# Splitting the last output stores of an attention and gated-MLP kernel

## The chip, the cores and the metric

The kernel runs on one core of a Trainium2 chip. The metric is the device time of one execution in microseconds. Three runs of the kernel before gave 410.19, 409.29 and 409.55 us, median 409.55.

## What is computed

For four sequences of 768 tokens, eight heads of width 64: softmax attention, in which a token sees 8 global positions and the 96 before it, with a bias that grows with distance. Its output x (512 wide) goes through a gated MLP, and x is added to the result:

```
h = gelu(x @ w_in)                       # 512 -> 1024, tanh form
u, v = h[..., :512], h[..., 512:]
v_n = (v - mean) / sqrt(var + 1e-6) * g_ln
v_s = w_sg @ v_n + b_sg                  # mixes the 768 tokens
out = x + (u * v_s) @ w_out              # float32
```

## The kernel before

The output is kept transposed: 512 rows (features) by 768 columns (tokens) for each sequence. `out_tile` makes one tile of it, 128 rows (feature block `m`, 0 to 3) by 384 columns (token chunk `c`, 0 or 1): 32 tiles in all. Matmuls work on float32 values split into a high and a low part, three for each of the four steps of the contraction (lines 547 to 549), and add up in a PSUM tile `mm_ps`. When the last step is done, VectorE adds x and writes the tile `o` in SBUF (line 670), and SyncE stores `o` with one DMA (line 676): 128 rows of 1,536 bytes. All stores and loads are issued by SyncE.

Each step is an `Op` of a plan. `Plan.order` simulates the engines with fixed costs (for a store: SP, 0.38 us) and a table of shifts, and writes the instructions of each engine down in that order, so an operation's callback may issue several instructions, but the plan counts only the costs that stand beside it.

The end of the kernel is the last sequence's second chunk, which is marked `last`. There x's two parts are added into `o` ahead (line 662), so that after the matmuls one add is left. Line 1326 sets the order: the steps of tiles `m` = 0, 1, 2 are interleaved, so that these three end one shortly after the other, and tile `m` = 3 follows on its own:

```
phase([], [t[k] for k in range(KD) for t in o[1][:3]] + o[1][3])
```

Behind the plan, line 1335 loads a flag on each engine and line 1336 branches over a general path that these inputs don't need. At that point SyncE waits for eight DMA counters, one wait each; the closing of the program (shown as line 1481) waits for eight again, and then all engines meet in a barrier.

Of the kernel before, what the change touches and what calls it, by code (L numbers as in the profile page):

```python
# [15 lines left out]
ALU = mybir.AluOpType  # L16
PSUM = bass.MemoryType.PSUM

P = 128
# [5 lines left out]
KD = DM // P  # L25
CH = 384
# [20 lines left out]

PATIENCE = 2.0

HINTED = ("DVE", 40, mybir.EngineType.DVE), ("PE", 30, mybir.EngineType.PE)  # L50

IDLE, ON_UNTIL = 0.3, 75.0
# [99 lines left out]
def on_dve(n, more=0.0):  # L152
    return "DVE", 0.065 + n / 960 + more, 0.155 + n / 960 + more


def on_dve_sb(n, more=0.0):

    return "DVE_SB", 0.065 + n / 960 + more, 0.155 + n / 960 + more
# [7 lines left out]
def on_pool(n, more=0.0):  # L166
    return "POOL", 0.05 + n / 390 + more, 0.08 + n / 390 + more
# [41 lines left out]
def parts(used):  # L209

    return [(b.buf, b.part) if isinstance(b, View) else b if isinstance(b, tuple) else (b, None)
            for b in used]
# [18 lines left out]
class Now:  # L231
# [5 lines left out]
    def op(self, ways, reads=(), writes=()):  # L237
        for b, _ in parts(writes):
            if b.kind and b.tile is None:
                n = self.next[b.kind] = self.next.get(b.kind, -1) + 1  # L240
                b.slot = n % self.places[b.kind]
        ways[0][-1]()


class Plan:
# [247 lines left out]
    def emit(self, start):  # L493
# [5 lines left out]
        todo = self.search(start)  # L499
        hinted = {[o for o in todo if o.way[0] == e][-n]: t for e, n, t in HINTED}  # L500
        for o in todo:
# [22 lines left out]
class Moe:  # L524
# [128 lines left out]
    def out_tile(self, x, c, m, dst, last=False):  # L653
        nc, w, op, gt = self.nc, self.w, self.plan.op, self.gt
        cs = slice(c * CH, (c + 1) * CH)
        ms = slice(m * P, (m + 1) * P)

        whole = self.temp("o", CH) if last else None

        def ahead(first):  # L660
            xm = x[m][c]
            both = lambda eng: eng.tensor_tensor(whole.ap, xm[:, 0, :].bitcast(F32),
                                                 xm[:, 1, :].bitcast(F32), ALU.add)
            op([on_dve_sb(CH) + (lambda: both(nc.vector),),
                on_pool(CH) + (lambda: both(nc.gpsimd),)], [xm], [whole], [first])

        def after(ps):
            o, xm = whole or self.temp("o", CH), x[m][c]
            with_x = lambda: o.ap if last else xm[:, 0, :].bitcast(F32)
            op([on_dve(CH) + (lambda: nc.vector.tensor_tensor(  # L670
                o.ap, ps.ap, with_x(), ALU.add),)], [ps, xm], [o])
            if not last:
                lo = lambda eng: eng.tensor_tensor(o.ap, o.ap, xm[:, 1, :].bitcast(F32), ALU.add)  # L673
                op([on_dve_sb(CH) + (lambda: lo(nc.vector),),
                    on_pool(CH) + (lambda: lo(nc.gpsimd),)], [xm], [o])
            op([("SP", 0.38, 0.7, lambda: nc.sync.dma_start(dst[ms, cs], o.ap))], [o], [])

        return self.terms(
            KD, CH, lambda k: ((w.wout[:, 0, k, ms], w.wout[:, 1, k, ms]),
                               (gt[c, k][:, 0, :], gt[c, k][:, 1, :])),  # L680
            lambda k: [gt[c, k], (w.wout, (k, m // 2))], 1, after, ahead if last else None)
# [803 lines left out]
```

## Time and profile before

| | |
|---|---|
| median of three runs | 409.55 us |
| the profiled execution | 409.76 us |
| its span, first to last instruction | 407.9 us |
| PE busy | 396.8 us (97%) |
| VectorE busy | 321.8 us (79%) |
| ScalarE busy | 216.8 us (53%) |
| output stores | 32, of 192 KB each |

Times inside the profile count from the start of the span. The rows come from one profiled execution. "SPq" is SyncE's queue of DMA issues and waits, which count as no busy time. A DMA's landing is the time from its issue until its counter says that all of it has arrived.

### The profile page before, as it was taken

The page shows a single profiled execution, that of the slowest core. Times are in us where ns is not written, and L with a number is a line of the kernel's source. Part 1 is how long each engine was busy: PE and PEld are TensorE (multiplying, and loading weights), DVE is VectorE, ACT ScalarE, POOL GpSimd, SP SyncE. Part 2 cuts the span into 40 slices and gives each one's busy share as a digit, 9 for nine tenths or more (in the row PEclk, how much of TensorE's full clock was granted, in tenths as well). Part 3 has the DMA queues.
Part 4 walks back from the last instruction along what each step waited for, and adds up shares of the span by engine and source line. Part 5 has one row for each costly group of instructions (what it writes and reads, how often), then busy time and mean ns, then how long its engine had stood idle before and what let it go on. Part 6 is the DMA issues. An engine that isn't in the chain of part 4 may idle for free.

```text
span 407.9 us, 12436 instructions
## 1 busy us (share of the span) xinstructions
PE 396.8 (97%) x4593; PEld 360.9 (88%) x4593; DVE 321.8 (79%) x1088; ACT 216.8 (53%) x726; POOL 184.0 (45%) x332
## 2 busy tenths in 40 slices
PE   7889999999999999999999999999999999999995
PEld 4667778899998989899999888999999888999995
DVE  7998999999978999877667899866667668764372
ACT  5999999875646855545333565642333234400110
POOL 3324553373557676666456445553456142403200
PEclk9999999999999999999999999999999999999998
DMA  7874765236777886655887872753676501001002
GB/s 232 282 221 129 216 209 147 95 106 209 244 240 224 256 271 203 183 165 168 252 241 237 249 233 82 202 147 129 190 240 189 168 19 40 0 2 57 23 0 82
DMA packets 50033, 67.12 MB, mean 165 GB/s; under 512 B 5808, under 2 KB 33968, under 8 KB 49968
## 3 DMA queue, kind: packets, MB, share of 16 engines
q1 hardware_dynamic: 49968, 66.28, 52.9%
q8 instruction: 37, 0.61, 0.6%
q14 instruction: 28, 0.23, 0.2%
HBM read 47.91 MB, written 18.35 MB: 162 GB/s over the span
## 4 chain that ended last, share of the span: by engine, by line
PE 85%; DVE 10%; issue 1%; DMA 1%; ACT 1%; POOL 0%; POOLq 0%
PE mm_ps L547 24%; PE mm_ps L549 23%; PE mm_ps L548 23%; PE av L1043 7%; PE s_ps L894 6%; PE tps L1015 2%; DVE p L926 1%; DVE stage L719 1%; DVE stage L717 1%; DMA stage<-in_w_in_dram 1%; DVE p L956 1%; DVE st L605 1%; DVE vg L571 1%; DVE win L724 1%; DVE stage L715 1%
## 5 line engine op out<-in xcount | busy, mean ns | idle before, releaser
L931 ACT ACTIVATE p<-p,pst 128x168 f32<-128x168 f32 (+1 forms) x192 | 80.9, 425 | 28.8 <-DVE pst L926 23.7
L953 POOL TENSOR_SCALAR p<-p,pst 128x168 f32<-128x168 f32 (+1 forms) x137 | 57.2, 434 | 27.8 <-DVE pst L944 27.4
L547 PE MATMUL mm_ps<-wsg,z 128*128 128x384 f32 x192 | 65.0, 339 | 0.0
L549 PE MATMUL mm_ps<-wsg,z 128*128 128x384 f32 x192 | 64.3, 335 | 0.1
L548 PE MATMUL mm_ps<-wsg,z 128*128 128x384 f32 x192 | 64.2, 334 | 0.0
L926 DVE CUSTOM_DVE_ANT_0 p<-s_ps,bias 128x168 f32<-128x168 f32 (+1 forms) x192 | 53.5, 318 | 6.7 <-PE s_ps L894 5.2
L673 POOL TENSOR_TENSOR o<-o,x 128x384 f32<-128x384 f32 x28 | 28.7, 1023 | 52.5 <-DVE o L670 39.0
L1043 PE MATMUL av<-pt,v 64*64 64x128 f32 (+1 forms) x1408 | 47.9, 251 | 1.4 <-DVE pt L1021 1.1
L1043 PEld LDWEIGHTS av<-pt,v 64*64 64x64 f32 x1408 | 36.8, 134 | 10.2 <-issue 5.3
L547 PE MATMUL mm_ps<-x,win 128*128 128x384 f32 x128 | 43.9, 343 | 0.0
L547 PE MATMUL mm_ps<-gt,wout 128*128 128x384 f32 x128 | 43.0, 336 | 0.0
L548 PE MATMUL mm_ps<-gt,wout 128*128 128x384 f32 x128 | 43.0, 336 | 0.0
L549 PE MATMUL mm_ps<-gt,wout 128*128 128x384 f32 x128 | 42.9, 335 | 0.0
L549 PE MATMUL mm_ps<-x,win 128*128 128x384 f32 x128 | 42.8, 335 | 0.0
L548 PE MATMUL mm_ps<-x,win 128*128 128x384 f32 x128 | 42.8, 334 | 0.0
L566 ACT ACTIVATE u<-mm_ps 128x384 f32<-128x384 f32 x32 | 15.6, 488 | 45.7 <-PE mm_ps L549 45.2
L547 PE MATMUL mm_ps<-win,x 128*128 128x512 f32 x96 | 39.5, 411 | 0.0
L894 PE MATMUL s_ps<-qk 64*64 64x64 f32 (+2 forms) x1408 | 39.0, 242 | 0.1
L549 PE MATMUL mm_ps<-win,x 128*128 128x512 f32 x96 | 37.7, 393 | 0.0
L548 PE MATMUL mm_ps<-win,x 128*128 128x512 f32 x96 | 37.7, 392 | 0.0
L894 PEld LDWEIGHTS s_ps<-qk 64*64 64x64 f32 x1408 | 34.0, 135 | 3.9 <-issue 2.7
L547 PEld LDWEIGHTS mm_ps<-wsg,z 128*128 128x128 f32 x192 | 36.0, 188 | 1.4 <-issue 0.9
(112 smaller groups left out, 900.7 us busy)
## 6 DMA issues: line engine op xcount, KB each, us to landing
qk<-in_qk_in_dram SPq DMA_DIRECT2D x32, 328.0 KB, 4.1
pt<-far SPq DMA_DIRECT2D x24, 384.0 KB, 4.8
v<-in_v_in_dram SPq DMA_DIRECT2D x32, 256.0 KB, 4.1
out_dram<-o SPq DMA_DIRECT2D x32, 192.0 KB, 2.2
far<-tt SPq DMA_DIRECT2D x48, 96.0 KB, 1.9
far<-stage SPq DMA_DIRECT2D x48, 96.0 KB, 2.3
qk<-in_qk_in_dram SPq DMA_DIRECT2D x16, 276.0 KB, 3.7
v<-in_v_in_dram SPq DMA_DIRECT2D x16, 192.0 KB, 4.1
```

What stands on the lines that cost most here:

```text
L547: mm(ps.ap, ah, bh, start=(i == 0), stop=False)
L548: mm(ps.ap, ah, bl, start=False, stop=False)
L549: mm(ps.ap, al, bh, start=False, stop=(i == n - 1))
L566: op([on_act(n) + (lambda: nc.scalar.activation(out.ap, h.ap, AF.Square, scale=math.sqrt(GELU_C * GELU_A)),)], [h], [out])
L571: op([on_dve(n) + (lambda: nc.vector.scalar_tensor_tensor(out.ap, out.ap, 1.0, h.ap, ALU.add, ALU.mult),)], [h], [out])
L673: lo = lambda eng: eng.tensor_tensor(o.ap, o.ap, xm[:, 1, :].bitcast(F32), ALU.add)
L894: nc.tensor.matmul(s_ps[h][e * HQ:(e + 1) * HQ, i * W + c0:i * W + c0 + n], qk[rows, qc:qc + HQ], qk[rows, QW + k0:QW + k0 + n], start=Tru ...
L926: nc.vector.tensor_tensor_reduce(out=p[:, g, cols], in0=s_ps[h][:, i * W:i * W + nk], in1=bias[:, 2 * j + h, w0:w0 + nk], op0=ALU.add, op1 ...
L931: op([on_act(nk, 0.225) + (lambda p=p, g=g, cols=cols, i=i: nc.scalar.activation(p[:, g, cols], p[:, g, cols], AF.Exp, bias=st[:, 0, i, g: ...
L953: op([on_pool_ts(nk, -0.10) + (partial(scaled, lambda o, a, c: nc.gpsimd.tensor_scalar(o, a, c, 1.0, ALU.mult, ALU.mult)),), on_act(nk, 0. ...
L1015: nc.tensor.transpose(tps[:, a * P:(a + 1) * P], pc[:, c:c + P], ident)
L1043: nc.tensor.matmul(to, v[rows, vc:vc + D], of, stop=True, skip_group_check=True, **kw)
```

## The change

The last tile (`m` = 3 of the last chunk of the last sequence, `ending`) is added in two instructions of 192 columns and stored in two DMAs of 192 columns, 128 rows of 768 bytes each. The stores of the other three tiles of that chunk are issued in parts by rows: tile 0 in three (rows 0 to 41, 42 to 84, 85 to 127), tiles 1 and 2 in two (64 rows each). All other tiles are added and stored as before. The costs that the planner sees are unchanged.

```diff
+STORED_IN = {0: 3, 1: 2, 2: 2}
...
             o, xm = whole or self.temp("o", CH), x[m][c]
             with_x = lambda: o.ap if last else xm[:, 0, :].bitcast(F32)
-            op([on_dve(CH) + (lambda: nc.vector.tensor_tensor(
-                o.ap, ps.ap, with_x(), ALU.add),)], [ps, xm], [o])
+            ending = last and m == KD - 1
+            some = [slice(0, CH // 2), slice(CH // 2, CH)] if ending else [slice(0, CH)]
+
+            def add():
+                for s in some:
+                    nc.vector.tensor_tensor(o.ap[:, s], ps.ap[:, s], with_x()[:, s], ALU.add)
+
+            def store():
+                for s in some:
+                    nc.sync.dma_start(dst[ms, c * CH + s.start:c * CH + s.stop], o.ap[:, s])
+
+            def in_parts(n):
+                for h in range(n):
+                    rows = slice(h * P // n, (h + 1) * P // n)
+                    nc.sync.dma_start(dst[m * P + rows.start:m * P + rows.stop, cs], o.ap[rows])
+
+            op([on_dve(CH) + (add,)], [ps, xm], [o])
...
-            op([("SP", 0.38, 0.7, lambda: nc.sync.dma_start(dst[ms, cs], o.ap))], [o], [])
+            op([("SP", 0.38, 0.7, partial(in_parts, STORED_IN[m]) if last and m in STORED_IN else store)], [o], [])
```

## Rows read from the trace of the kernel before

**Rows 1.** The page: span, busy time of the engines, chain by engine.

```profile
span 407.9 us, 12436 instructions
...
PE 396.8 (97%) x4593; PEld 360.9 (88%) x4593; DVE 321.8 (79%) x1088; ACT 216.8 (53%) x726; POOL 184.0 (45%) x332
...
PE 85%; DVE 10%; issue 1%; DMA 1%; ACT 1%; POOL 0%; POOLq 0%
```

**Rows 2.** Timeline of the last adds: start, duration (us), instruction, [idle before].

```profile
400.33 1.60 DVE L670 TENSOR_TENSOR o<-mm_ps,o 128x384 f32<-128x384 f32 x3 [2.24 <-PE mm_ps L549]
...
403.08 0.34 PE L549 MATMUL mm_ps<-gt,wout 128*128 128x384 f32 x1
403.45 0.56 DVE L670 TENSOR_TENSOR o<-mm_ps,o 128x384 f32<-128x384 f32 x1 [1.06 <-PE mm_ps L549]
```

**Rows 3.** Timeline of SyncE: the four stores of the last chunk.

```profile
400.92 0.33 SPq L676 DMA_DIRECT2D out_dram<-o  x1
...
401.44 0.33 SPq L676 DMA_DIRECT2D out_dram<-o  x1
...
401.96 0.33 SPq L676 DMA_DIRECT2D out_dram<-o  x1
...
404.04 0.33 SPq L676 DMA_DIRECT2D out_dram<-o  x1
```

**Rows 4.** DMA view of 404.5 to 406: 40 slices (busy tenths, GB/s), packets by queue.

```profile
DMA  0000000000786979969799764105700000000000
GB/s 0 0 0 0 0 0 0 0 0 0 287 328 246 573 287 410 451 246 614 287 369 492 287 206 123 41 0 219 218 0 0 0 0 0 0 0 0 0 0 0
DMA packets 146, 0.21 MB, mean 142 GB/s; under 512 B 16, under 2 KB 144, under 8 KB 144
...
q1 hardware_dynamic: 144, 0.20, 35.4%
q14 instruction: 2, 0.02, 3.3%
```

**Rows 5.** Line 676: issues (ns min/median/max) of all stores, then of the last chunk.

```profile
L676 SPq DMA_DIRECT2D out_dram<-o x32: 332/344/1202, 107.6 to 404.0; - x32
...
L676 SPq DMA_DIRECT2D out_dram<-o x4: 332/332/333, 400.9 to 404.0; - x4
...
DMA to landing us min/median/max: 1.9/1.9/2.1
```

**Rows 6.** Lines 1336 and 1481: SyncE's waits at the end, first and last start.

```profile
L1336 SPq EVENT_SEMAPHORE  x2: 17/17/17, 404.9 to 405.0; - x2
...
L1336 SPq EVENT_SEMAPHORE  x6: 17/17/17, 406.2 to 406.5; - x6
...
L1481 SPq EVENT_SEMAPHORE  x8: 28/28/28, 406.6 to 407.0; - x8
...
L1481 SPq EVENT_SEMAPHORE  x10: 17/28/28, 406.6 to 407.8; - x10
```

**Rows 7.** Timeline of SyncE near 314: four issues in a row, and the first.

```profile
314.32 1.75 SPq L990 DMA_DIRECT2D far<-tt  x4
...
314.32 0.30 SPq L990 DMA_DIRECT2D far<-tt  x1
```

**Rows 8.** Groups by form, VectorE: adds of two widths; busy us, mean ns.

```profile
L1119 DVE TENSOR_TENSOR x<-av,x 128x128 fp32r<-128x128 f32 x56 | 12.7, 282 | 0.1
...
L670 DVE TENSOR_TENSOR o<-mm_ps,o 128x384 f32<-128x384 f32 x4 | 2.2, 558 | 3.3 <-PE mm_ps L549 3.3
```

**Rows 9.** Stretches while the last four stores transfer; the last columns are DMA share, GB/s.

```profile
core 0: us, PE busy (x) PEld busy (x) DVE busy (x) ACT busy (x) POOL busy (x), PEclk, DMA share, GB/s
...
402.50:403.00 0.50, 0.50 (x5) 0.50 (x4) 0.00 (x0) 0.00 (x0) 0.00 (x0) 1.00 1.02 372
...
405.00:405.30 0.30, 0.00 (x0) 0.00 (x0) 0.00 (x0) 0.00 (x0) 0.00 (x0) 1.00 1.03 389
```

**Rows 10.** A stretch in which only rows of 768 bytes are transferred (as before).

```profile
315.50:316.00 0.50, 0.50 (x8) 0.25 (x6) 0.39 (x1) 0.00 (x0) 0.00 (x0) 1.00 0.83 206
```

## The prediction

> **What bounds the kernel now.** I read the page's engine totals first: PE is busy for 396.8 us of a 407.9 us span, and PE lines make up 85% of the chain of waits [rows 1]. Then the end of that chain, since the change touches nothing before it: the last matmuls and one VectorE add, which ends at 403.45 + 0.56 = 404.01 [rows 2]. There the chain as listed stops, but the span goes on for 3.9 us. The other views say what fills it. SyncE issues the last store at 404.04 [rows 3]. Its packets start about 0.83 us later: in the DMA slices of 404.5 to 406 (each 0.0375 us wide) the first busy one begins at 404.87, and the store's packets end about 405.5 [rows 4]. The slowest of the four stores takes 2.1 us from issue to landing, so it has landed at about 404.04 + 2.1 = 406.14 [rows 5]. SyncE waits at the kernel's end for eight counters, one after another: two of these waits are over by 405.0, six run off only from 406.2 to 406.5; then eight more and the closing barrier go to 407.9 [rows 6]. So the last 4 us are add, issue, transfer, landing, waits, barrier, each on the path. No matmul is left to hide anything, and whatever store lands last sets the time.
>
> The span stands in an execution of 409.76 us; the median of the runs shown is 409.55. I sum against the profiled one and take off the 0.21 at the end.
>
> **The change, part by part.**
>
> *More issues on SyncE.* Four stores become nine. A store issued after a wait takes 0.33 us [rows 3]; issues that follow one another at once are slower: four in a row take 1.75 us, the first 0.30, so (1.75 - 0.30)/3 = 0.48 a step [rows 7]. I take 0.38 for the first step (0.33 and a gap of 0.05) and 0.48 for the rest; 0.38 for all is the other end. The parts of tile 0 are issued at 400.92, 401.30 and 401.78, those of tiles 1 and 2 from 402.26 to 403.70, and SyncE is free at 404.18 instead of waiting for the last add. The add itself: a 128x384 add takes 558 ns and a 128x128 one of the same operation 282 ns [rows 8], so 1.08 ns a column and 351 ns for 192 columns. Adds back to back step by (1.60 - 0.56)/2 = 0.52 us [rows 2], so by 0.52 - 0.21 = 0.31 at half width. The second half ends 0.31 + 0.35 = 0.66 us after the start, 0.10 later than now, the first half 0.21 earlier. Behind these adds VectorE has only its share of the ending. The halves of tile 3 go out at 404.18 and 404.66, so the last issue is 0.62 later than 404.04. With 0.38 a step SyncE is free in time and the last issue is at about 404.22, 0.18 later.
>
> *Transfers.* Between 405.0 and 405.3 the 16 engines carry 389 GB/s with nothing idle, 24.3 GB/s each, so a row of 1,536 bytes takes 63 ns (66 by the 372 GB/s of 402.5 to 403.0) [rows 9]. Rows of 768 bytes, in the stage of the small transfers, run at 206 GB/s with a share of 0.83: 206/0.83/16 = 15.5 GB/s, 50 ns a row [rows 10]. Half the columns is not half the time: 8 half-rows take 0.40 us against 0.50 for 8 whole ones.
>
> *How the rows are shared out.* This decides. The last store shows 144 packets, of which 16 are under 512 bytes: 128 rows and one closing packet for each of 16 engines, and with all 16 busy to the end these are equal shares of 8 rows [rows 4, 9]. Tile 0 is now cut at rows 42 and 85, into 42, 43 and 43 rows. No transfer of the trace has such a count, so I bound it. Spread over 16 engines as now, 43 rows are at most 3 rows an engine, 0.19 us. On one engine they are 43 x 63 ns = 2.7 us, twice. Which row is nearer? What the rows show is equal shares, and 43 is prime: it has no equal share below 43 engines except all on one. I take the upper end, and keep the lower for the range.
>
> By the row alone, read as "always 16 engines", the sum would be about +0.1 us. The Trainium skill ("DMA: Bandwidth & Descriptors", section "Why a DMA increments its semaphore by 16 and not by 1") speaks against this change: a store from SyncE runs on the largest number of engines, up to 16, that divides the count of the slowest dimension on both sides, and 127 partitions go to one engine. By it 42 rows go to 14 engines and 43 to one, which gives the sum below; no run here shows it, since every count in the trace divides by 16.
>
> *The sum with one engine for each 43-row part.* I assume that both parts go to the same engine, and that this one also has its share of every later store, in order of issue. It starts at 401.30 + 0.83 = 402.13 (its share of the 42 rows is done by then). It carries 86 rows (5.42 us), 4 of 64 rows from each of four parts of tiles 1 and 2 (16 x 63 ns = 1.01) and 8 half-rows from each half of tile 3 (16 x 50 ns = 0.80): 7.23 us, so it is done at 409.36. The late issues above are covered by this queue, and so is the slower add. From the last packet to the landing I take 0.44: a landing of 1.9 us, the median of the four [rows 5], would have come at 405.94, after packets that end about 405.5. Landing at 409.80 against 406.14: +3.66.
>
> *The waits at the end.* The counters are taken in turn, and the wait on the last store is now third of eight; five more stores would make it the eighth. The five waits behind it, of (406.5 - 406.2)/5 = 0.06 us each or a little more by the rounded row [rows 6], are then over before the landing; I take 0.33. That stores take the counters in the order of the waits is inferred; otherwise this is 0.
>
> Sum: +3.66 - 0.33 = +3.33. 409.76 + 3.33 - 0.21 = 412.88; the 63 ns may hold moments in which an engine had not started, so I round down to 412.8. Its own range: 60 ns a row (-0.3), if the 63 hold such starts, gives 412.5; 66 ns a row (+0.3) and a landing of 0.77 after the last packet, as the store of 2.1 us would have it (+0.33), give 413.5.
>
> **Rivals.**
>
> *All 16 engines share any count* (not slower). Then 42 or 43 rows cost what they cost now, the first store's data leave a little earlier to no use, and the end is set by SyncE: last issue 0.62 later, its rows 0.10 shorter, five waits fewer (0.33): +0.19; with 0.38 a step (0.18 in place of 0.62) it is -0.25. Between them 409.3 to 409.75, about 409.5: no change. Instruction fetches run beside the last store (two packets of another queue, [rows 4]), and the landing of 2.1 against 1.9 may be theirs; free of them it is 0.2 less, 409.1. For it: 389 GB/s shows that the sharing works well. Against it: nothing shows unequal shares. It decides at about 31 rows: an engine with fewer of tile 0's last two parts than that (31 x 63 ns + the 1.81 of the later stores = 3.76 us from 402.13) is done by 405.89, when the last half-rows would be anyway (404.66 + 0.83 + 0.40).
>
> *The pile-up also blocks the issue.* One store of this line took 1.20 us to issue against a median of 0.34 [rows 5], so SyncE can be held up. If it is held until the full engine has drained, the last halves start a first-packet delay later: 0.83 more, 413.6. For it: 86 rows are far more than any engine has queued in the ending now. Against it: an engine that always has work loses nothing by a late issue, and SyncE needs to be ahead by one part only.
>
> *The halves don't work as halves.* If the first half's store waited for both adds, it would be issued at 403.45 + 0.66 + 0.03 = 404.14, when SyncE is not yet free. Worth nothing in either case.
>
> **How the numbers follow.** One engine for 43 rows 0.64 (412.8), the same with blocked issue 0.08 (413.6), shared by 16 0.22 (409.5), something that the rows don't show 0.06. A measurement of this kernel can tell about 0.2%, 0.82 us, from no change. The first two are slower; the third stays within 0.82 us on both sides, even with the 0.2 of the fetches; a gain of 0.82 us is in no sum, 0.05 of the rest. The range runs from the rival's 409.1 to 413.6.
>
> **What the profile after would show.** Right: DMA share near one sixteenth, some 24 GB/s, for several us after 403; a landing of over 5 us for stores of line 676's successor; SyncE's last wait at about 409.8 and none after it before the final eight; VectorE done at about 404.1 and PE unchanged. Wrong: the DMA share falls to zero by 406, all landings near 2 us; then the shares are not equal ones. If the last wait is still followed by five of 0.07 us, the order of counters was wrong. Matmuls that move before 403 would mean that the plan changed, which I exclude: the costs handed to the planner are the same.

## The result and the profile after

The changed kernel takes 413.7 us (median of 5 runs, 413.41 to 413.9) against 409.55 us: ratio 1.0093, 95% interval 1.0078 to 1.0109. The two medians are 4.15 us apart (a ratio of 1.0101, inside the interval, which in us runs from 3.2 to 4.5). The forecast was 412.8, and its range ended at 413.6, 0.1 below the result. The profiled execution took 413.7 us with a span of 411.9 us, 4.0 more than before.

Everything up to the last adds is as before: the first add starts at 400.4 against 400.33 [rows 2]. The difference lies behind. First the adds (line 676 is the old 670), then SyncE's timeline (start, duration; line 685 issues the parts by rows, line 680 the whole stores and the halves of columns):

```profile
L676 DVE TENSOR_TENSOR o<-mm_ps,o x5: 347/556/559, 400.4 to 403.8; 128x384 f32<-128x384 f32 x3, 128x192 f32<-128x192 f32 x2
```

```profile
401.02 3.70 SPq L685 DMA_DIRECT2D out_dram<-o  x7
...
401.47 0.24 SPq L685 DMA_DIRECT2D out_dram<-o  x1
...
404.81 1.05 SPq L680 DMA_DIRECT2D out_dram<-o  x2
...
405.47 0.40 SPq L680 DMA_DIRECT2D out_dram<-o  x1
```

The adds are as forecast: 347 ns at half width. SyncE hardly pauses between 401.02 and 405.87, and its last issue is 1.43 us later than before [rows 3], not 0.62. Next the DMA view from 401 to 411 (40 slices of 0.25 us) and three stretches of the windows view (last columns: DMA share, GB/s):

```profile
DMA  0004410010978688836759685411100000000000
GB/s 0 0 0 123 117 37 12 12 18 0 86 49 80 123 221 289 264 98 160 172 114 216 211 261 175 122 52 40 40 25 25 25 25 25 22 25 15 0 0 0
```

```profile
402.30:403.10 0.80, 0.80 (x6) 0.80 (x6) 0.19 (x1) 0.00 (x0) 0.00 (x0) 1.00 0.08 19
403.10:404.40 1.30, 0.42 (x3) 0.10 (x1) 0.62 (x2) 0.00 (x0) 0.00 (x0) 1.00 0.56 48
...
408.50:410.20 1.70, 0.00 (x0) 0.00 (x0) 0.00 (x0) 0.00 (x0) 0.00 (x0) 0.50 0.07 24
```

Read the right end of the GB/s line: from 408.25 to 410 the kernel stores at 22 to 25 GB/s with a DMA share of 0.07, one sixteenth. That is one engine at full pace while fifteen have nothing left; before, the stores still ran at 389 GB/s from 405.0 to 405.3, shortly before their end [rows 9]. Last, SyncE's waits in the stretches 406 to 408, 408.5 to 409.2 and 409.2 to 412 (line 1352 is the old 1336), and the row parts (ns of an issue, first and last start; then us to landing, which this view has for the four parts of 64 rows). The last line shown is line 1497, the old 1481, from 410.55 on:

```profile
L1352 SPq EVENT_SEMAPHORE  x1: 17/17/17, 406.4 to 406.4; - x1
...
L1352 SPq EVENT_SEMAPHORE  x1: 17/17/17, 409.0 to 409.0; - x1
...
L1352 SPq EVENT_SEMAPHORE  x6: 17/17/17, 409.3 to 410.5; - x6
```

```profile
L685 SPq DMA_DIRECT2D out_dram<-o x7: 242/536/587, 401.0 to 404.1; - x7
...
DMA to landing us min/median/max: 5.9/6.4/7.0
```

```profile
L1497 SPq EVENT_SEMAPHORE  x10: 17/28/28, 410.6 to 411.9; - x10
```

The waits pass one by one as the stores land behind each other: first 43-row part at 406.4, second at 409.0, the other six counters until 410.5. The first 43-row part needed 4.9 us from its issue at 401.47, the second 2.6 us more, which is 43 rows at 61 ns. And after the wait at 410.5 the closing eight begin at once (410.6): the last store's counter is now last in the row.

### The profile page after: what moved, and what is told of

Its sections match the earlier page's. It is cut to its first block, busy times and chain, and to the rows that moved or that the text cites. A ratio compares the mean times of both kernels' runs of the same rounds, so it can differ in the third digit from the quotient of the medians.

```text
span 411.9 us, 12443 instructions
## 1 busy us (share of the span) xinstructions
PE 397.2 (96%) x4593; PEld 361.1 (88%) x4593; DVE 321.8 (78%) x1089; ACT 216.8 (53%) x726; POOL 183.7 (45%) x332
## 4 chain that ended last, share of the span: by engine, by line
```

## The experiments

Each variant was timed beside the kernel before on the same chip, the last one with a single execution of each; ratios are to it, and differences in us are between medians. N stands for the kernel before without its branch. "Landings with data" are read from the trace: a store's counter is updated once for each engine that carries rows, when they have landed. If fewer than 16 engines carry rows, one update more comes 0.4 to 0.5 us after the issue starts, before any row has landed (43 rows: updates at 401.88 and 406.35 for the issue at 401.47).

**Tile 0 in 48, 48 and 32 rows.** In all row variants the parts are named by the rows at which they are cut:

```diff
-STORED_IN = {0: 3, 1: 2, 2: 2}
+STORED_IN = {0: (48, 96), 1: (64,), 2: (64,)}
-            def in_parts(n):
-                for h in range(n):
-                    rows = slice(h * P // n, (h + 1) * P // n)
-                    nc.sync.dma_start(dst[m * P + rows.start:m * P + rows.stop, cs], o.ap[rows])
+            def in_parts(cuts):
+                for a, e in zip((0,) + cuts, cuts + (P,)):
+                    nc.sync.dma_start(dst[m * P + a:m * P + e, cs], o.ap[a:e])
```

> Tile 0 in 48, 48 and 32 rows instead of 42, 43 and 43; all else as in the changed kernel, nine stores. If a store is shared in equal parts among engines (theory: a count that divides by 16 goes to 16 engines, 43 to one), no engine has more than 9 rows of tile 0 and the pile-up is gone: last landing near 407, all landings 2 to 2.5 us, time 409.5 to 410.2, so 3.5 to 4.2 us below the changed kernel. Rival 1, the nine issues on SyncE (0.4 to 0.59 us each) and the smaller pieces cost the time: 413 or more, as the changed kernel. Rival 2, half-height parts (64 rows) are slow in themselves: 411 to 413, with packets of several hundred ns.

411.85 us, ratio 1.0049 (1.0037 to 1.0061), a miss: of 4.15 us lost 1.9 are gone, 2.2 remain. The time lies in the range of rival 2, slow parts of 64 rows, and their rows are slow, though not by several hundred ns: 174 GB/s at a share of 0.73 (line below) is 14.9 GB/s an engine, 103 ns a row in place of 63. Without the branch (below) they are as slow (145 GB/s at 0.60 in the same stretch), yet 1.3 of the 2.2 us are gone, so slow rows don't explain these. The row parts landed in 1.6 to 2.8 us, so the pile-up is gone; but the two last halves took 3.5 and 3.9 us, and the waits show them (line 680: the halves; line 1351: SyncE's waits from 407.9 on; DMA packets by queue from 401 to 411; the stretch of the 64-row parts):

```profile
DMA to landing us min/median/max: 3.5/3.7/3.9
```

```profile
L1351 SPq EVENT_SEMAPHORE  x2: 17/17/17, 409.1 to 409.4; - x2
```

```profile
q1 hardware_dynamic: 784, 0.79, 29.5%
q8 instruction: 1, 0.02, 1.0%
q14 instruction: 2, 0.02, 0.7%
```

```profile
404.50:405.50 1.00, 0.00 (x0) 0.00 (x0) 0.00 (x0) 0.00 (x0) 0.00 (x0) 1.00 0.73 174
```

In the trace's landings 15 of the 16 shares of the last half are in by 407.75, and one comes at 409.3. On the instruction queues a fetch of 16 KB starts at 406.34 and takes 1.68 us, another of 8 KB follows at 407.56. That suggested a second mechanism: a store that is late meets instruction fetches on one engine.

**Tile 0 in 44, 42 and 42 rows.** As above with `0: (44, 86)`.

> Tile 0 in 44, 42 and 42 rows: no count is a multiple of 16, but 44 divides by 11 and 42 by 14. Equal shares: 11 and 14 landings with data instead of 16, 3 or 4 rows an engine, time as with 48, 48, 32 within 0.3 us (409.5 to 410.3). If only counts that divide by 16 are shared and all others go to one engine: 128 rows on one engine, 415 to 416.

411.74 us, ratio 1.0051 (1.0036 to 1.0065), the same as with 48, 48, 32, and like that run above the 409.5 to 410.3 expected. The trace has 11, 14 and 14 landings with data for the three parts. So it is not multiples of 16 that count: in all counts tried here the rows go to the largest number of engines up to 16 that divides them.

**Tile 0 alone.** `STORED_IN = {0: (42, 85)}`, and `ending = False`: the last tile is whole.

> Only tile 0 in 42, 43 and 43 rows; tiles 1, 2 and 3 are stored whole and the last add is one instruction: six stores. Theory (one engine has 86 rows, then 24 more of the whole tiles): from about 402.3, 110 rows at 61 to 63 ns make 6.8 us, last landing near 409.5, three waits behind it (0.2 us): time 412.6 to 413.0. If the engine is held up again for some 0.9 us, as in the changed kernel, 413.5 to 413.9. Rival 1, number of issues: six in place of nine, so 409.8 to 411.

413.83 us, ratio 1.0101 (1.0087 to 1.0116): six stores cost as much as nine, so the number of issues is not what sets the changed kernel's time; and the first 43-row part is held up here too (4.9 us to landing).

**Columns alone.** `STORED_IN = {}`; the last tile is added and stored in halves.

> Only the last tile's add and store in halves of the columns, no parts by rows: five stores. The second half is issued at about 404.2 to 404.3, 0.2 later than the whole store before; 8 rows of 768 bytes at 33 ns (as the trace after has them at one engine) make 0.27 in place of 0.50; one wait fewer behind the last landing (0.07): 409.2 to 409.6, no change that can be told. If halves of columns were part of the loss: above 410.4.

410.61 us, ratio 1.0021 (1.0013 to 1.003): a miss. I had expected no change, and it costs 0.98 us between the medians (0.5 to 1.2 by the interval). The first half lands in 1.6 us, the second in 2.6: one engine's share comes at 406.77, the other fifteen by 405.87, beside three fetches.

**The counters.** Four whole stores at the end; the stores of the chunk before are cut in nine.

```diff
+EARLY_IN = {0: (48, 96), 1: (64,), 2: (64,), 3: (64,)}
...
+            op([("SP", 0.38, 0.7, partial(in_parts, EARLY_IN[m]) if early and m in EARLY_IN else ...
```

> The ending as in the kernel before (four whole stores, one add); instead the four stores of the chunk before it are issued in 3, 2, 2 and 2 parts (48, 48, 32 and 64 rows), five more stores long before the end. Theory of the counters (taken in turn by the stores, waited for in a fixed order): the wait on the last store moves from third to last of eight, the five waits behind it are over earlier, span shorter by 0.3 to 0.4 us, time about 409.2 against 409.6. Rival, the order is not that of the stores: no change in the waits, time within 0.1 us of before.

409.21 us, ratio 0.9988 (0.9979 to 0.9997): 0.1 to 0.9 us less, which holds the 0.3 to 0.4 of the waits. In its profile one wait is left from 405.9 on, at 406.0, where the kernel before had six [rows 6]:

```profile
L1352 SPq EVENT_SEMAPHORE  x1: 17/17/17, 406.0 to 406.0; - x1
```

So stores take the eight counters in turn (in the trace the last store's counter is the third that is waited for in the kernel before, the eighth here), and the waits behind the last store are saved when its counter is the last in the row. This version is 0.12% faster than the kernel before, which the interval separates from none only just.

**Without the branch.** Three runs, and the two after them, leave out the path for other window sizes (unused with these inputs) and the two hints for it, so that no branch fetches instructions at the end. This also takes away the branch's eight waits, from N as from the variants:

```diff
-    flag = nc.values_load(general[0:1, 0:1], min_val=0, max_val=1)
-    with tc.If(flag == 1, label="general"):
-        dense_path(tc, future, ng, nl, iota, w, (q_t, k_t, v_n), out)
```

The kernel before (N):

> The kernel before without the branch to the general path and without the two hints for it (left out: the path for other window sizes). No instruction fetch of a branch at the end. Serves as the base N of the next two. Expected 0.3 to 1.5 us below the kernel before, since eight waits belong to the branch.

408.8 us, ratio 0.998 (0.9971 to 0.9989). Columns alone:

> Columns alone (the last tile added and stored in two halves of 192 columns), without the branch and its hints as in N. With the branch this cost 0.98 us. Theory: instruction fetches of the branch (8 and 16 KB on one DMA engine) hold up the share of that engine of the late second half; without them N - 0.2 to N + 0.3. Rival, halves of columns are slow in themselves: N + 0.8 to N + 1.1.

408.5 us: N - 0.3, where it was +0.98 with the branch. Parts of 48, 48, 32, 64 and 64 rows and halved columns:

> Tile 0 in 48, 48 and 32 rows, tiles 1 and 2 in 64, columns halved, nine stores, without the branch and its hints as in N. With the branch this cost 2.2 us. Theory: issues of 0.4 to 0.6 us each on SyncE make the last store 1.4 to 1.5 us late, which is all that is left without the fetches: N + 0.9 to N + 1.5. Rival, the fetches have no part in it: N + 2.0 to N + 2.4.

409.72 us: N + 0.92, where it was +2.2. Its last half is issued 1.64 us later than N's last store and lands 1.44 later; it has fewer waits behind it. Both variants fall by 1.3 us relative to their base, and both lose the late share. The DMA view of the last halves of columns alone, with the branch (404.4 to 406.9), then without (404.2 to 406.7):

```profile
DMA  0002899851048997200050001900000000000000
...
q8 instruction: 1, 0.02, 3.5%
q14 instruction: 2, 0.02, 2.7%
...
out_dram<-o SPq DMA_DIRECT2D x1, 96.0 KB, 2.6
```

```profile
DMA  0005999620179995100000000000000000000000
...
q1 hardware_dynamic: 288, 0.20, 23.6%
...
out_dram<-o SPq DMA_DIRECT2D x1, 96.0 KB, 1.6
```

With the fetches the second half lands in 2.6 us, without them in 1.6.

**The changed kernel without the branch.**

> The changed kernel (42, 43 and 43 rows, 64 and 64, columns halved) without the branch to the general path and its hints, as in N (408.8). Theory: the one engine with 86 more rows than its share ends the kernel, and the fetches are on other engines or lie beside its queue: N + 3.8 to N + 4.3. Rival, the changed kernel's loss is fetches and late issues as with 48, 48, 32: N + 0.9 to N + 1.5.

412.88 us: N + 4.08 (the kernel before was 0.16 faster in this job than in that of N, so 4.1 to 4.2). The fetches cost the changed kernel nothing that shows: its second 43-row part lands 2.65 us behind the first with them, 2.64 without, so they are not in that engine's way. In the DMA view of 401 to 411 its end is the same plateau of 25 GB/s:

```profile
GB/s 0 0 135 105 37 12 12 18 0 92 55 68 123 240 277 252 111 135 154 129 169 181 274 218 98 25 25 25 25 25 25 25 25 25 22 9 0 0 0 0
```

**A smaller dose.** `0: (43,)`, tile 0 in 43 and 85 rows, without the branch.

> Tile 0 in 43 and 85 rows, tiles 1 and 2 in 64, columns halved, eight stores, without the branch and its hints. Equal shares: 43 rows on one engine, 85 rows as 17 on each of five, so the fullest engine has 60 rows of tile 0 in place of 89 (42/14 + 86). From about 401.8: 60 rows (3.7 us), 16 rows (1.0), 16 half-rows (0.53), landing 0.35 later, near 407.4: N + 1.1 to N + 1.4. If the engine is held up for some 0.9 us again when the next stores begin: N + 1.9 to N + 2.3. Rival, 85 rows also on one engine: N + 3.5 or more. Landings with data: 1 and 5.

410.82 us: N + 2.02. There are 1 and 5 landings with data, and the 43-row store took 4.8 us to land. So the loss grows with the rows of tile 0 on the fullest engine (8 rows N + 0.92, 60 rows N + 2.02, 89 rows N + 4.08), and the hold-up of about 0.9 us is there with one such store as well.

**The same rows far from the end.** `EARLY_IN = {0: (42, 85), ...}`, ending as before.

> As e_early_five, but the early tile 0 is cut in 42, 43 and 43 rows in place of 48, 48 and 32; the ending is four whole stores. Theory: the same 86 rows go through one engine, 5.3 us at 61 ns a row, but far from the end nothing waits for them: time as e_early_five (409.2) within 0.2 us, landings of 3 to 7 us for the two parts. Rival, a 43-row store costs time wherever it stands: 411 or more.

409.16 us, ratio 0.9988 (0.9979 to 0.9997), as with 48, 48, 32 in the same place. The first 43-row store again took 4.7 us, the second landed 2.6 later, and nothing waited for them.

**127 rows on one engine.** `EARLY_IN = {0: (127,), 1: (42, 85), 2: (64,), 3: (64,)}`, one execution.

> As i_early_43, but the early tile 0 is cut in 127 rows and 1, early tile 1 in 42, 43 and 43, tiles 2 and 3 in 64 and 64. In four runs the first 43-row store on its engine took 4.7 to 4.9 us to land, 0.9 to 1.1 more than 0.83 + 43 x 61 ns + 0.35; the one right behind it took 2.65 more, no excess. If the excess is a fixed cost at the start of a one-engine store: 127 rows land after 0.83 + 7.8 + 0.35 + 1.0 = 10.0 us. If it is a slower pace of every row of such a store (84 instead of 61 ns): 11.8 us. Time as e_early_five within 0.3 us in either case.

409.54 us beside 409.60 for the kernel before. The store of 127 rows landed after 9.7 us: 0.7 more than its rows at 61 ns explain, not 2.8. So the excess is a cost near the start of a one-engine store, not a pace. Its packets show where it lies: of the first 16 rows, from 373.13 on, five take 129 to 314 ns, which with a slower first one makes 0.75 us; from 374.87 on each row starts 61 ns behind the one before. No row of another store moves in this stretch, only one fetch of 8 KB at 373.61, which is in the first line here:

```profile
373.00:374.80 1.80, 1.80 (x12) 1.80 (x11) 0.28 (x2) 0.00 (x0) 1.01 (x1) 1.00 0.08 18
374.80:376.00 1.20, 1.20 (x9) 1.20 (x8) 0.49 (x1) 0.00 (x0) 0.63 (x1) 1.00 0.06 24
```

The issues behind the full engine were blocked (line 685; ns of an issue, min/median/max):

```profile
L685 SPq DMA_DIRECT2D out_dram<-o x9: 268/541/2543, 372.3 to 382.0; - x9
```

## Why the prediction was right, and what it got wrong

**The step that decides held.** 43 rows go to one engine, and what it carries ends the kernel. Landings with data (1 for 43 and 127 rows, 5 for 85, 11 for 44, 14 for 42) show it, and so does the plateau at a sixteenth. They agree with the rule of the Trainium skill ("DMA: Bandwidth & Descriptors", "Why a DMA increments its semaphore by 16 and not by 1") in every count tried. Cutting tile 0 at 48 and 96 instead gave back 1.9 us with the branch and 3.2 without (412.88 - 409.72); the difference is what the fetches cost the version in 48, 48 and 32, and the pile-up hides. Of the signs named ahead, the share of one sixteenth came, but alone only for 1.75 us, from 408.25 on; before that other engines still had rows.

**The sum was 0.9 us short, and the term that was too small is that of the 86 rows: the sum had no hold-up of the first one-engine store.** By its terms, in the profiled execution, the last landing came at 410.5, 0.7 later than the 409.80 of the sum.
- The 86 rows: 5.42 forecast. From 402.30 (issue 401.47 + 0.83) to the second part's last packet at 408.64 it is 6.34, +0.92. The second part ran at 61 ns a row; the first 43 rows were held up by about 1 us. This is the mis-sized term. The sum's own upper end, 413.5, allowed for 66 ns a row and 0.77 us to landing, and both came out smaller (61 ns, 0.34 us). The windows view shows the stretch: 19 GB/s at 402.3 to 403.1, then 48 GB/s over all engines until 404.4.
- The start of the engine: the first 43-row part was issued at 401.47, not 401.30, +0.17, of which 0.10 is the whole ending's shift.
- The 16 rows and 16 half-rows behind: 1.81 forecast, 1.5 between the waits at 409.0 and 410.5. The half-rows take 33 ns here, not the 50 of the small transfers [rows 10].
- Last packet to landing: 0.34 in place of 0.44, -0.10.
- The waits: the closing eight follow the last landing at once, as forecast (0.33 saved), and the early variant shows the mechanism alone.
- The base: 409.76 against 409.55, which I took off, was not there after (413.7 both), +0.21. The forecast had also been rounded down from 412.88.

**Late issues and the slower add** were covered by the queue, as said. But SyncE's steps were 0.29 to 0.68 us, the long ones from the 64-row parts on, not 0.48 throughout.

**The rival of 16 engines** was priced wrongly. 409.5 was its forecast (with +0.1 in another place, where its own sums gave -0.25 to +0.19); an evenly shared version takes 411.85. Without the branch, with late issues and nine stores, it is N + 0.92; 1.3 more go with the branch, where one engine's share is late. I had taken the fetches as 0.2 that could be won. In the profiles the last share comes behind the other fifteen by 0.25 us when the last store is issued at 404.04 (kernel before), 0.90 at 404.20 (columns alone), 0.94 at 405.13 (44, 42, 42) and 1.59 at 405.80 (48, 48, 32), in one execution each. Blocked issue does occur, up to 2.5 us behind 127 rows, but not behind two parts of 43 in the changed kernel (0.59 at most; 1.0 with 43 and 85 rows). Its added 0.83 was not what brought the time to 413.7: that its 413.6, the end of the range, lies so near is chance.

**Left open:** what holds up the first rows of a one-engine store for 0.7 to 1 us. It is neither the fetches (it stays without the branch) nor the ending (it stays far from it) nor the rows of the next stores (127 rows were alone when it happened); nothing here shows its cause. And that a fetch and the late share sit on the same engine is inferred from their times and from its going away with the branch; the records don't name the engine. The times fit closely: in columns alone a fetch that starts at 405.24 ends at 405.80, and the eight late rows begin at 405.79; with 48, 48, 32 the 16 KB end at 408.02, and the late rows begin at 408.00.

## What to carry to other kernels

When a store or load is cut in parts, cut it at rows that give every part a count with a large divisor up to 16 (32, 48 or 64, also 42 or 44, not a prime such as 43 or 127), and look at the number of landings with data. At the end of a kernel more parts are more issues, and a store that slips by 0.2 us, as with columns alone, can run into the instruction fetches of the closing branch. Where a store's counter stands in the order of the last waits is worth 0.3 to 0.4 us here, and can be set by stores issued before, as the early ones were, about 30 us before the end.

## What the runs showed of the hardware that was not expected

- A store on one engine starts slowly: 4.7 to 4.9 us to land for 43 rows in the changed kernel, with 43 and 85 rows, and far from the end, where 0.83 + 2.64 + 0.35 = 3.8 were expected; the next store behind it runs at 61 ns a row. With 127 rows the whole excess lies in a few of the first 16 rows.
- Rows of 768 bytes take 33 ns on an engine in these stores, 50 in the scattered transfers of the same size [rows 10].
- Stores of 64 rows were issued at 0.53 to 0.60 us each, whole stores of 128 rows after a pause at 0.33 [rows 3] and close behind another store at 0.37 (tile 0 alone). Rows of the 64-row parts took 103 ns on an engine in the version in 48, 48 and 32, of whole stores 63 [rows 9].
- Fetches of 8 and 16 KB beside the last store delayed one sixteenth of it by 0.9 us (columns alone) to 1.6 us (48, 48, 32), in one execution each; that they share its engine is inferred.
